# Cosformer attention into a SwiGLU layer on one core: the order of the opening's products, the gates of two load groups, and later loads of q for batch 3

## The chip, the cores and the metric

The kernel runs on one core of a Trainium2 chip. The metric is the device time of one execution in microseconds (us). Before the change it is 332.5 us, the median of 12 runs (331.68 to 333.79).

## What is computed

Attention with linear cost over 8 batches of 8 heads, 576 tokens and 64 features, and then a gated layer on all 4608 tokens:

```python
def phi(x, c, s):
    r = np.maximum(x, 0.0)
    return np.concatenate([r * c, r * s], axis=-1)   # c, s: cosine and sine of the token's place
q_p = phi(q, cos_w, sin_w); k_p = phi(k, cos_w, sin_w)
kv = np.einsum('bhsf,bhsd->bhfd', k_p, v); z = np.sum(k_p, axis=2)
num = np.einsum('bhsf,bhfd->bhsd', q_p, kv)
den = np.einsum('bhsf,bhf->bhs', q_p, z)[..., None] + 1e-06
x = num / den                        # heads side by side: 4608 x 512
xn = x / np.sqrt(np.mean(x * x, -1) + 1e-06) * rms_g
g = xn @ w_gate; val = xn @ w_val    # 512 x 1536
out = (g * sigmoid(g) * val) @ w_out # 1536 x 512
```

## The kernel before, in words

**Stages of a batch.** The 512 first tokens of a batch are handled as four tiles of 128 (the index c or j), the other 64 as a tail (index 4; tails of two batches are joined). `k_phi` and `q_phi` (L219, L231) apply phi on VectorE (V, the cosine half) and ScalarE (A, the sine half). `v_cast` and `v_cast_tail` copy v into bf16, the tail on GpSimd (G). `kvz_pe` (L294) forms kv and z for all heads in the PSUM tile psA, and `kvz_evac` copies them out. phi(q) is transposed, on TensorE with a copy behind it (`q_tr_pe`, `q_tr_evac`, L259, L265) for batches 0 and 1, by a transposing DMA on SyncE's queue for the others (`q_tr_dma`, L254). `nd_pe` (L322) forms numerator and denominator of one tile in psA. `nd_post` (L374) divides them on VectorE. `x_sq` (L389) sums the squares on ScalarE and takes the power -1/2 on GpSimd (rs). `x_norm` (L403) scales on VectorE. x is transposed on TensorE (`x_tr_pe`, `x_tr_evac`, L426, L432) or by DMA (`x_tr_dma`, L423).

**The gated layer.** A block is the 512 first tokens of one batch; a ninth block holds all tails. Block blk has 12 steps n = 0 to 11 (`gval_step`, L715): four products each with w_gate and w_val of 128 output features (`gval_mm`, L440), an activation on ScalarE (`gval_act`), a product on VectorE (`gval_h`, L456). Then come four steps n = 12 to 15 of twelve products with w_out (`out_step`, L724), each copied by ScalarE and stored. psG and psV have two banks each, so TensorE may run one step ahead.

**Order.** Every engine runs its instructions in the order of the program. That order is written out by hand: `at(blk, n, where, f, ...)` (L638) hangs a call into a step, before its products ("pe"), in the middle of them ("mid"), before its activation ("pre") or behind it ("post"). While block b is computed, batch b+1 goes through attention. x of batch 2 is normalised and transposed behind its nd at steps 7, 9, 11 and 12 of block 1 (`nds`, L689). Loads of batch 3 and later are cut in pieces and hung into the steps of the block two earlier (L707 to L713), between the transposing DMAs on SyncE's queue.

**The opening** (L489 to L624). TensorE multiplies a tile of zeros (`filler`, L482) where it has nothing yet. Batch 0 goes through attention tile by tile, and steps 0 to 5 of block 0 are computed in parts of 128 or 256 columns (`open_ffn`, L560, each group of four products accumulating one bank part; `open_h`, L575) as soon as a tile of x is there. Steps 6 to 11 follow (L737). Then the twelve w_out products of all four tiles of block 0 are run together, n by n, with the attention of batch 1 between them (L747 to L779); the product number n needs quarter n // 3 of wo.

**Loads and their gates.** w_gate and w_val are loaded in three slices of columns each by GpSimd's queue (`weight_dmas` 0 to 5, L497 to L506). k, q and v of batch 1 come on SyncE's queue behind weights 4 (L645 to L651). wo comes in four quarters on GpSimd's queue: the first waits for k of batch 1, the second for q of batch 1 (L652 to L657). The q tails of batches 0 and 1 wait for the third quarter, and k, q and v of batch 2 stand behind them on SyncE's queue (L761 to L767).

Of the kernel before, what the change touches and what calls it, by code (L numbers as in the profile page):

```python
# [22 lines left out]
def kernel(  # L23
# [40 lines left out]
    LOW, HIGH = (0, 4), (4, 8)  # L64
# [200 lines left out]
    def q_tr_evac(eng, b, c, bank, heads=(0, 8)):  # L265
        h0, h1 = heads if c < 4 else (0, 4)
        dst = bank.bitcast(BF16).rearrange("p (h s) -> p h s", s=P)
        copy(eng, q_dst(b, c)[:, h0:h1, :], dst[:, h0:h1, :])
# [105 lines left out]
    def nd_post(b, j, pst):  # L374
        o = headview(pst)
        xt = x_tile(b, j)
        rec = four.tile([P, 2, 4], FP32, name="rec", tag="rec")
        nc.vector.tensor_scalar(
            out=rec[:, :, :], in0=o[:, :, :, D], scalar1=1e-6, scalar2=None, op0=ALU.add
        )  # L380
        nc.vector.reciprocal(out=rec[:, :, :], in_=rec[:, :, :])
        nc.vector.tensor_tensor(  # L382
            out=xt[:, 0:DM].rearrange("p (b h d) -> p b h d", b=2, d=D),
            in0=o[:, :, :, 0:D],
            in1=rec[:, :, :].unsqueeze(3).to_broadcast([P, 2, 4, D]),
            op=ALU.mult,
        )

    def x_sq(b, j):  # L389
        xt = x_of[(b, j)]  # L390
        scr = one.tile([P, DM + 1], BF16, name="scr", tag="scr")
        ms = four.tile([P, 1], FP32, name="ms", tag="ms")
        nc.scalar.activation(  # L393
            out=scr[:, :], in_=xt[:, 0 : DM + 1], func=AF.Square,
            scale=1.0 / math.sqrt(DM), accum_out=ms[:, :],
        )
        rs = four.tile([P, 1], FP32, name="rs", tag="rs")
        nc.gpsimd.tensor_tensor(out=rs[:, :], in0=ms[:, :], in1=mhalf[:, :], op=ALU.pow)  # L398
        rs_of[(b, j)] = rs
# [3 lines left out]
    def x_norm(b, j):  # L403
        xn = four.tile([P, DM], BF16, name="xn", tag="xn")
        nc.vector.scalar_tensor_tensor(  # L405
            out=xn[:, :], in0=x_of[(b, j)][:, 0:DM], scalar=rs_of[(b, j)][:, :], in1=gb[:, :],
            op0=ALU.mult, op1=ALU.mult,
        )
        xn_of[(b, j)] = xn
# [16 lines left out]
    def x_tr_pe(b, j, bank):  # L426
        xn = xn_of[(b, j)]
        dst = bank.bitcast(BF16).rearrange("p (t s) -> p t s", s=P)
        for t in range(NDT):
            nc.tensor.transpose(dst[:, t, :], xn[:, t * P : (t + 1) * P], ident[:, :])  # L430

    def x_tr_evac(eng, b, j, bank, part=(0, 4)):  # L432
        dst = bank.bitcast(BF16).rearrange("p (t s) -> p t s", s=P)
        copy(eng, x_dst(b, j)[:, part[0] : part[1], :], dst[:, part[0] : part[1], :])
# [47 lines left out]
    def filler(n, bank):  # L482
        for _ in range(n):
            nc.tensor.matmul(bank, lhsT=warm[:, 0:P], rhs=warm[:, :], start=True, stop=True)  # L484
# [75 lines left out]
    def open_ffn(pair, steps, c0, c1, base=0, parts=(0, 1)):  # L560

        x = xnT[0]
        for i, n in enumerate(steps):
            for a in parts:
                w = (wg, wv)[a]
                bank = pairs[pair][a]
                lo = base + 256 * i + c0 % 256
                for t in range(NDT):
                    nc.tensor.matmul(  # L569
                        bank[:, lo : lo + c1 - c0],  # L570
                        lhsT=w[:, t, n * P : (n + 1) * P], rhs=x[:, t, c0:c1],
                        start=(t == 0), stop=(t == NDT - 1),
                    )
# [17 lines left out]
    x_norm(0, 1)  # L591
    open_ffn(0, (0, 1), 0, 128)
    x_tr_pe(0, 1, psV[1][:, :])
    x_tr_evac(A, 0, 1, psV[1][:, :])
    q_tr_evac(V, 0, 3, psO[1][:, :])
    nd_pe(0, 2, psA)
    nd_post(0, 2, psA)
    x_sq(0, 2)
    filler(2, psG[1][:, :])
    open_ffn(0, (0, 1), 128, 256)  # L600
    open_ffn(1, (2, 3), 0, 256, parts=(0,))
    nd_pe(0, 3, psA)
    nd_post(0, 3, psA)
    x_norm(0, 2)
    open_ffn(2, (4, 5), 0, 256, parts=(0,))
    open_h(0, 0, 0)
    x_sq(0, 3)
    x_tr_pe(0, 2, psA[:, 0, :])
    x_tr_evac(A, 0, 2, psA[:, 0, :])
    open_ffn(1, (2, 3), 0, 256, parts=(1,))  # L610
    x_norm(0, 3)
    open_h(1, 2, 0)
    open_ffn(2, (4, 5), 0, 256, parts=(1,))
    open_ffn(0, (0, 1), 256, 384)
    x_tr_pe(0, 3, psA[:, 1, :])
    x_tr_evac(A, 0, 3, psA[:, 1, :])
    open_h(2, 4, 0)
    filler(1, psA[:, 0, :])
    open_ffn(0, (0, 1), 384, 512)
    open_h(0, 0, 1)  # L620
    open_ffn(1, (2, 3), 256, 512)
# [28 lines left out]
    load_main("v", v, 1, HIGH)  # L650
    load_tail("v", v, 1)  # L651
    w = wo_load(0)  # L652
    tc.add_manual_dep(w.ins, d.ins.name, SYNC_DEP, reason="after k of batch 1")
    w = wo_load(1)
    tc.add_manual_dep(w.ins, gate_q.ins.name, SYNC_DEP, reason="after q of batch 1")
    wo_load(2)
# [1 line left out]


    for c in range(5):  # L660
        at(0, 8 + c // 3, "post", k_phi, V, 1, c, 0)
        at(0, 8 + c // 3, "post", k_phi, A, 1, c, 1)
    for c in range(3):
        at(0, 10 + c // 2, "post", q_phi, V, 1, c, 0)
        at(0, 10 + c // 2, "post", q_phi, A, 1, c, 1)
    at(0, 11, "post", v_cast_tail, G, 1)


    for nb in range(2, B):
        b = nb - 1  # L670
        late = nb == 2
        vb, vn = (b, 3) if late else (b - 1, 14)
        if late:
            at(vb, vn, "post", v_cast, V, nb, LOW)
        for c in range(5):
            kb, kn = (b, (1, 1, 1, 1, 2)[c]) if late else (b - 1, 12 + (c * 3) // 5)
            if not late or c > 1:
                at(kb, kn, "post", k_phi, V, nb, c, 0)
            if not late or c > 0:
                at(kb, kn, "post", k_phi, A, nb, c, 1)  # L680
            qn = (2, 3, 5, 5, 6)[c] if late else c
            at(b, qn, "post", q_phi, V, nb, c, 0)
            at(b, qn, "post", q_phi, A, nb, c, 1)
            at(b, qn, "post", q_tr_dma, nb, c)
        if not late:
            at(vb, vn, "post", v_cast, V, nb, LOW)
        at(vb, vn + 1, "post", v_cast, V, nb, HIGH)
        at(vb, vn, "post", v_cast_tail, G, nb)
        kz, nds = (6, (7, 9, 11, 12)) if late else (4, (5, 7, 9, 11))  # L689
        at(b, kz, "pe", kvz_pe, nb, psA)  # L690
        at(b, kz, "pre", kvz_evac, A, nb, psA, 0)
        at(b, kz, "pre", kvz_evac, A, nb, psA, 1)
        for j in range(4):
            n = nds[j]
            at(b, n, "mid" if n == NNT else "pe", nd_pe, nb, j, psA)
            at(b, n, "pre", nd_post, nb, j, psA)
            at(b, n, "post", x_sq, nb, j)
            where = "pre" if n + 1 >= NNT else "post"
            at(b, n + 1, where, x_norm, nb, j)
            at(b, n + 1, where, x_tr_dma, nb, j)  # L700
        if nb % 2 == 1:
            at(b, 13, "pe", nd_pe, nb, 4, psA)
            at(b, 13, "pre", nd_post, nb, 4, psA)
            at(b, 13, "post", x_sq, nb, 4)
            at(b, 14, "post", x_norm, nb, 4)
            at(b, 14, "post", x_tr_dma, nb, 4)
    for nb in range(3, B):  # L707

        b = nb - 2
        for i, which in enumerate(("k", "v", "q")):  # L710
            for p in range(5):
                n = (0, 6, 10)[i] + p if b == 1 else 5 * i + p
                at(b, n, "post", load_piece, which, nb, p)  # L713

    def gval_step(blk, n, bank=None):  # L715
        bank = n % 2 if bank is None else bank
# [25 lines left out]
        x_tr_pe(1, j, bank)  # L742
        x_tr_evac(A, 1, j, bank)

    qbank = [psA[:, 0, :], psV[0][:, :], psV[1][:, :], psA[:, 0, :]]
    nd_at = {4: 0, 6: 1, 8: 2, 9: 3}
    for n in range(NNT - 2):  # L747
        for c in ((0, 1), (2,), (3,))[n] if n < 3 else ():
            q_tr_pe(1, c, qbank[c])
            q_tr_evac(V if c % 2 else A, 1, c, qbank[c])  # L750
        if n == 0:
            q_phi(V, 1, 3, 0)
            q_phi(A, 1, 3, 1)
        if n == 1:
            v_cast(A, 1, LOW)
            v_cast(V, 1, HIGH)
        if n == 3:
            kvz_pe(1, psA)
            kvz_evac(A, 1, psA, 0)
            kvz_evac(V, 1, psA, 1)  # L760
            for bb in (0, 1):  # L761
                d = load_tail("q", q, bb)
                if bb == 0:
                    tc.add_manual_dep(d.ins, wo_dmas[2].ins.name, SYNC_DEP, reason="after wo")
            load("k", 2)
            load("q", 2)
            load("v", 2)  # L767
        if n == 7:
            x_norm(1, 0)
        if n == 9:  # L770
            x_norm(1, 1)
            tr1(0, psV[0][:, :])
        if n in nd_at:
            j = nd_at[n]
            nd_pe(1, j, psA)
            nd_post(1, j, psA)
            x_sq(1, j)
        for j in range(4):
            out_mm(0, j, n, banks0[j])  # L779
# [89 lines left out]
```

## Time and profile before

| | us |
|---|---|
| median of 12 runs | 332.5 |
| the profiled execution | 332.48 |
| its span in the trace | 330.3 |
| TensorE busy in the span | 320.7 |
| VectorE, ScalarE, GpSimd busy | 181.6, 168.5, 37.7 |
| first step of block 0 with 512 columns (n = 6) starts | 34.13 |
| first w_out product of block 0 | 45.39 |
| block 1 starts, with half of the columns | 60.07 |
| block 2 starts | 96.29 |

The trace gives the start and length of every instruction in us from the start of the span, and, in brackets, how long the engine stood idle before it and what ended that. A row "x8" is eight instructions in a chain; their ends overlap, so the price of one is read from the start of the next row: four products of 512 columns take 0.86, four of 256 columns 0.44, four of 128 columns 0.22, the eight of an nd 0.26, one filler 0.22. L74 and L85 are lines of load helpers, L255 and L424 the transposing DMAs of phi(q) and of x, L272 and L274 copies on ScalarE and on VectorE or GpSimd, L474 the store of an output tile.

### The profile page before, as it was taken

The page shows a single profiled execution, that of the slowest core. Times are in us where ns is not written, and L with a number is a line of the kernel's source. Part 1 is how long each engine was busy: PE and PEld are TensorE (multiplying, and loading weights), DVE is VectorE, ACT ScalarE, POOL GpSimd, SP SyncE. Part 2 cuts the span into 40 slices and gives each one's busy share as a digit, 9 for nine tenths or more (in the row PEclk, how much of TensorE's full clock was granted, in tenths as well). Part 3 has the DMA queues.
Part 4 walks back from the last instruction along what each step waited for, and adds up shares of the span by engine and source line. Part 5 has one row for each costly group of instructions (what it writes and reads, how often), then busy time and mean ns, then how long its engine had stood idle before and what let it go on. Part 6 is the DMA issues. An engine that isn't in the chain of part 4 may idle for free.

```text
span 330.3 us, 5951 instructions
## 1 busy us (share of the span) xinstructions
PE 320.7 (97%) x2191; PEld 163.7 (50%) x2191; DVE 181.6 (55%) x376; ACT 168.5 (51%) x326; POOL 37.7 (11%) x83
## 2 busy tenths in 40 slices
PE   8988999999989999999999999999999999999995
PEld 3567555654435444544454445444544444444443
DVE  3775576877755774577257755674567234204410
ACT  4554593785556556645564466536654233223321
POOL 3520311101200111012001110120001000000000
PEclk9999999999999999999999999999999999999999
DMA  7999997999699966876678777967631310020013
GB/s 209 282 192 254 307 198 223 321 198 222 155 268 206 193 167 191 209 173 194 203 165 202 180 216 186 197 154 238 134 67 32 116 45 0 2 110 17 0 34 96
DMA packets 95117, 54.14 MB, mean 164 GB/s; under 512 B 60016, under 2 KB 90480, under 8 KB 95088
## 3 DMA queue, kind: packets, MB, share of 16 engines
q1 hardware_dynamic: 89072, 48.65, 58.1%
q0 software_dynamic: 4768, 4.72, 8.7%
q10 hardware_dynamic: 1248, 0.39, 0.6%
q8 instruction: 17, 0.28, 0.3%
q14 instruction: 12, 0.10, 0.1%
HBM read 38.01 MB, written 9.44 MB: 144 GB/s over the span
## 4 chain that ended last, share of the span: by engine, by line
PE 86%; DVE 5%; DMA 4%; issue 2%; ACT 2%; POOL 0%; SPq 0%; ACTq 0%; DVEq 0%
PE psG L444 25%; PE psV L444 25%; PE psC L464 23%; PE psA L300 3%; DMA rq<-in_q_dram 2%; PE psA L328 2%; PE psG L464 1%; DVE xt L382 1%; DMA xnT<-xn 1%; PE psG L569 1%; DVE xn L405 1%; PE psV L569 1%; PE psO L569 1%; PE psG L484 1%; ACT scr L393 1%
## 5 line engine op out<-in xcount | busy, mean ns | idle before, releaser
L459 DVE TENSOR_TENSOR hT<-psV,sg 128x512 bf16<-128x512 f32 x102 | 70.3, 690 | 98.6 <-PE psV L444 87.3
L453 ACT ACTIVATE sg<-psG 128x512 f32<-128x512 f32 x102 | 60.6, 594 | 67.0 <-PE psG L444 66.8
L444 PE MATMUL psG<-xnT,wg 128*128 128x512 bf16 (+1 forms) x368 | 92.7, 375 | 1.5 <-DMA xnT<-xn 1.4
L444 PE MATMUL psV<-xnT,wv 128*128 128x512 bf16 (+1 forms) x368 | 92.7, 375 | 0.0
L464 PE MATMUL psC<-wo,hT 128*128 128x512 bf16 x396 | 89.4, 380 | 0.0
L444 PEld LDWEIGHTS <-wv 128*128 128x128 bf16 x416 | 40.6, 98 | 47.4
L464 PEld LDWEIGHTS <-hT 128*128 128x128 bf16 x420 | 40.2, 98 | 46.4
L444 PEld LDWEIGHTS <-wg 128*128 128x128 bf16 x416 | 38.5, 98 | 42.4 <-issue 1.9
L398 POOL TENSOR_TENSOR rs<-ms,mhalf 128x1 f32<-128x1 f32 x36 | 19.8, 549 | 191.0 <-ACT scr L393 191.0
L272 ACT COPY osb<-psC 128x512 f32<-128x512 f32 (+1 forms) x33 | 19.1, 578 | 43.5 <-PE psC L464 42.8
L393 ACT ACTIVATE scr<-xt 128x513 bf16<-128x513 f32 x36 | 22.8, 635 | 26.3 <-DVE xt L382 25.7
L405 DVE SCALAR_TENSOR_TENSOR xn<-xt,rs,gb 128x512 bf16<-128x512 f32 x36 | 27.3, 757 | 15.0 <-POOL rs L398 14.9
L382 DVE TENSOR_TENSOR xt<-psA,rec 128x512 f32<-128x512 f32 x35 | 24.2, 691 | 1.2
L213 ACT ACTIVATE qp<-rq,tab 128x512 bf16<-128x512 f32 x32 | 22.6, 714 | 1.3 <-DMA rq<-in_q_dram 1.2
L213 ACT ACTIVATE kpm<-rk,tab 128x512 bf16<-128x512 f32 (+1 forms) x34 | 21.2, 676 | 0.5 <-DMA rk<-in_k_dram 0.4
L215 DVE TENSOR_SCALAR kpm<-rk,tab 128x512 bf16<-128x512 f32 (+1 forms) x38 | 15.5, 460 | 4.3 <-ACT tab L168 3.3
L215 DVE TENSOR_SCALAR qp<-rq,tab 128x512 bf16<-128x512 f32 x32 | 15.1, 478 | 0.9 <-DMA rq<-in_q_dram 0.9
L484 PE MATMUL psG<-warm 128*128 128x512 bf16 x50 | 14.4, 434 | 1.2 <-DVE fidx L150 1.2
L328 PEld LDWEIGHTS <-qpT 128*128 128x128 bf16 x248 | 11.9, 98 | 6.9 <-issue 0.6
L328 PE MATMUL psA<-kvzs,qpT 128*128 128x65 bf16 x248 | 12.9, 194 | 0.2
L444 PE MATMUL psG<-xnt_tail,wg 128*128 128x512 bf16 x48 | 12.3, 380 | 0.0
L444 PE MATMUL psV<-xnt_tail,wv 128*128 128x512 bf16 x48 | 12.3, 379 | 0.0
(98 smaller groups left out, 194.1 us busy)
## 6 DMA issues: line engine op xcount, KB each, us to landing
out_dram<-osb SPq DMA_DIRECT2D x32, 256.0 KB, 2.5
rk<-in_k_dram SPq DMA_DIRECT2D x20, 256.0 KB, 3.3
rv<-in_v_dram SPq DMA_DIRECT2D x20, 256.0 KB, 3.1
rq<-in_q_dram SPq DMA_DIRECT2D x20, 256.0 KB, 3.2
rk<-in_k_dram SPq DMA_DIRECT2D x2, 1024.0 KB, 7.1
rq<-in_q_dram SPq DMA_DIRECT2D x2, 1024.0 KB, 9.5
rv<-in_v_dram SPq DMA_DIRECT2D x3, 512.0 KB, 9.9
wo<-in_moe_w_out_dram POOLq DMA_DIRECT2D x4, 384.0 KB, 8.6
```

The costliest lines, as they stand in the source:

```text
L213: nc.scalar.activation(out=out_ap, in_=in_ap, func=AF.Relu, scale=scale)
L215: eng.tensor_scalar(out=out_ap, in0=in_ap, scalar1=scale, scalar2=0.0, op0=ALU.mult, op1=ALU.max)
L272: nc.scalar.copy(out=o, in_=i)
L328: nc.tensor.matmul(o[:, g, i, :], lhsT=qpT[(b, 0)][:, h, j * P : (j + 1) * P], rhs=kvzs[(b, g)][:, i * E : (i + 1) * E], start=True, stop= ...
L382: nc.vector.tensor_tensor(out=xt[:, 0:DM].rearrange("p (b h d) -> p b h d", b=2, d=D), in0=o[:, :, :, 0:D], in1=rec[:, :, :].unsqueeze(3). ...
L393: nc.scalar.activation(out=scr[:, :], in_=xt[:, 0 : DM + 1], func=AF.Square, scale=1.0 / math.sqrt(DM), accum_out=ms[:, :],)
L398: nc.gpsimd.tensor_tensor(out=rs[:, :], in0=ms[:, :], in1=mhalf[:, :], op=ALU.pow)
L405: nc.vector.scalar_tensor_tensor(out=xn[:, :], in0=x_of[(b, j)][:, 0:DM], scalar=rs_of[(b, j)][:, :], in1=gb[:, :], op0=ALU.mult, op1=ALU. ...
L444: nc.tensor.matmul(pst[bank][:, cols[0] : cols[1]], lhsT=w[:, t, n * P : (n + 1) * P], rhs=x[:, t, cols[0] : cols[1]], start=(t == 0), sto ...
L453: nc.scalar.activation(out=sg[:, :], in_=psG[bank][:, :], func=AF.Silu)
L459: nc.vector.tensor_tensor(out=hTs[blk][:, n, :], in0=psV[bank][:, :], in1=sg[:, :], op=ALU.mult)
L464: nc.tensor.matmul(bank, lhsT=hTs[blk][:, n, j * P : (j + 1) * P], rhs=wo[:, n, :], start=(n == 0), stop=(n == NNT - 1),)
```

## The change

Five things, all in the order of work.

In the opening, the emptying of the transposes of q tile 3 and x tile 1 swap engines, one filler of two goes, nd of tile 3 moves ahead of the first products of steps 2 and 3, the second half of those products moves ahead of the transposes of x tile 2, the products of columns 256 to 384 move behind the transposes of x tile 3, and the filler there goes.

The first quarter of wo waits for the last weights instead of k of batch 1. The q tails, with batch 2's loads behind them, wait for the second quarter of wo instead of the third.

In batch 1, phi of k and q moves back by up to one step of block 0, and the transposes of q move from ahead of the w_out products n = 0, 1, 2 to ahead of n = 1 to 4.

In batch 3, the five pieces of q are loaded from step 13 of block 1 to step 1 of block 2 instead of steps 10 to 14 of block 1. Its q_phi and transposes come two steps later, and its nd one step later.

```diff
     x_tr_pe(0, 1, psV[1][:, :])
-    x_tr_evac(A, 0, 1, psV[1][:, :])
-    q_tr_evac(V, 0, 3, psO[1][:, :])
+    q_tr_evac(A, 0, 3, psO[1][:, :])
+    x_tr_evac(V, 0, 1, psV[1][:, :])
     nd_pe(0, 2, psA)
     nd_post(0, 2, psA)
     x_sq(0, 2)
-    filler(2, psG[1][:, :])
+    filler(1, psG[1][:, :])
     open_ffn(0, (0, 1), 128, 256)
-    open_ffn(1, (2, 3), 0, 256, parts=(0,))
     nd_pe(0, 3, psA)
     nd_post(0, 3, psA)
+    open_ffn(1, (2, 3), 0, 256, parts=(0,))
     x_norm(0, 2)
     open_ffn(2, (4, 5), 0, 256, parts=(0,))
     open_h(0, 0, 0)
     x_sq(0, 3)
+    open_ffn(1, (2, 3), 0, 256, parts=(1,))
     x_tr_pe(0, 2, psA[:, 0, :])
     x_tr_evac(A, 0, 2, psA[:, 0, :])
-    open_ffn(1, (2, 3), 0, 256, parts=(1,))
     x_norm(0, 3)
     open_h(1, 2, 0)
     open_ffn(2, (4, 5), 0, 256, parts=(1,))
-    open_ffn(0, (0, 1), 256, 384)
     x_tr_pe(0, 3, psA[:, 1, :])
     x_tr_evac(A, 0, 3, psA[:, 1, :])
     open_h(2, 4, 0)
-    filler(1, psA[:, 0, :])
+    open_ffn(0, (0, 1), 256, 384)
     open_ffn(0, (0, 1), 384, 512)
...
     w = wo_load(0)
-    tc.add_manual_dep(w.ins, d.ins.name, SYNC_DEP, reason="after k of batch 1")
+    tc.add_manual_dep(w.ins, weight_dmas[5].ins.name, SYNC_DEP, reason="after the weights")
...
     for c in range(5):
-        at(0, 8 + c // 3, "post", k_phi, V, 1, c, 0)
-        at(0, 8 + c // 3, "post", k_phi, A, 1, c, 1)
-    for c in range(3):
-        at(0, 10 + c // 2, "post", q_phi, V, 1, c, 0)
-        at(0, 10 + c // 2, "post", q_phi, A, 1, c, 1)
+        at(0, 8 + (c + 1) // 3, "post", k_phi, V, 1, c, 0)
+        at(0, 8 + (c + 1) // 3, "post", k_phi, A, 1, c, 1)
+    for c in range(2):
+        at(0, 11, "post", q_phi, V, 1, c, 0)
+        at(0, 11, "post", q_phi, A, 1, c, 1)
...
-            qn = (2, 3, 5, 5, 6)[c] if late else c
+            qn = (2, 3, 5, 5, 6)[c] if late else c + 2 * (nb == 3)
...
-        kz, nds = (6, (7, 9, 11, 12)) if late else (4, (5, 7, 9, 11))
+        kz, nds = (6, (7, 9, 11, 12)) if late else (4, (6, 8, 10, 12) if nb == 3 else (5, 7, 9, 11))
...
-                n = (0, 6, 10)[i] + p if b == 1 else 5 * i + p
-                at(b, n, "post", load_piece, which, nb, p)
+                n = (0, 6, 13)[i] + p if b == 1 else 5 * i + p
+                at(b + n // 16, n % 16, "post", load_piece, which, nb, p)
...
-    qbank = [psA[:, 0, :], psV[0][:, :], psV[1][:, :], psA[:, 0, :]]
+    qbank = [psV[0][:, :], psV[1][:, :], psV[0][:, :], psV[1][:, :]]
     nd_at = {4: 0, 6: 1, 8: 2, 9: 3}
     for n in range(NNT - 2):
-        for c in ((0, 1), (2,), (3,))[n] if n < 3 else ():
-            q_tr_pe(1, c, qbank[c])
-            q_tr_evac(V if c % 2 else A, 1, c, qbank[c])
         if n == 0:
-            q_phi(V, 1, 3, 0)
-            q_phi(A, 1, 3, 1)
-        if n == 1:
-            v_cast(A, 1, LOW)
-            v_cast(V, 1, HIGH)
+            for c in (2, 3):
+                q_phi(V, 1, c, 0)
+                q_phi(A, 1, c, 1)
         if n == 3:
             kvz_pe(1, psA)
             kvz_evac(A, 1, psA, 0)
             kvz_evac(V, 1, psA, 1)
+        if 1 <= n <= 4:
+            c = n - 1
+            q_tr_pe(1, c, qbank[c])
+            q_tr_evac(V if c < 2 else A, 1, c, qbank[c])
+        if n == 2:
+            v_cast(A, 1, LOW)
+            v_cast(V, 1, HIGH)
+        if n == 3:
             for bb in (0, 1):
                 d = load_tail("q", q, bb)
                 if bb == 0:
-                    tc.add_manual_dep(d.ins, wo_dmas[2].ins.name, SYNC_DEP, reason="after wo")
+                    tc.add_manual_dep(d.ins, wo_dmas[1].ins.name, SYNC_DEP, reason="after wo")
```

## The prediction

> **What bounds the kernel now.** I read the page's busy rows first, then TensorE's waits, then those waits in the timelines of TensorE, SyncE and VectorE, and last the transfers of the opening.
>
> ```profile
> PE 320.7 (97%) x2191; PEld 163.7 (50%) x2191; DVE 181.6 (55%) x376; ACT 168.5 (51%) x326; POOL 37.7 (11%) x83
> ...
> PEclk9999999999999999999999999999999999999999
> ```
>
> TensorE is busy for 320.7 of 330.3 us at the full granted clock. So only work taken off TensorE, or one of its waits, can be gained. These are all its waits:
>
> ```profile
> PE psG L444 <- DMA xnT<-xn: 1.4, 1, 1.4
> PE psG L484 <- DVE fidx L150: 1.2, 1, 1.2
> PE psA L430 <- DVE xn L405: 1.0, 1, 1.0
> PE psA L484 <- ACT xnT L272: 0.7, 1, 0.7
> PE psO L263 <- DVE qp L215: 0.6, 1, 0.6
> PE psV L263 <- ACT qp L213: 0.4, 1, 0.4
> ```
>
> The change can reach three: 1.0 and 0.7 in the opening, 1.4 at the start of block 2. In TensorE's timeline (start, us, then the wait in brackets):
>
> ```profile
> 25.60 0.40 PE L430 MATMUL psA<-ident,xn 128*128 128x128 bf16 x4 [1.01 <-DVE xn L405]
> ...
> 29.53 0.38 PE L484 MATMUL psA<-warm 128*128 128x512 bf16 x1 [0.67 <-ACT xnT L272]
> 29.75 0.39 PE L569 MATMUL psG<-xnT,wg 128*128 128x128 bf16 x4
> ```
>
> SyncE's queue ahead of the 1.4 us (the transposes L424 at 89.72 and 92.18 are those of tiles 2 and 3 of batch 2; loads of q for batch 3 stand before each), and VectorE's normalised tile 3, done at 90.11:
>
> ```profile
> 87.29 2.33 SPq L74 DMA_DIRECT2D rq<-in_q_dram  x2
> 89.72 1.23 SPq L424 DMA_TRANSPOSE xnT<-xn  x1
> 91.06 0.55 SPq L474 DMA_DIRECT2D out_dram<-osb  x1
> 91.66 0.42 SPq L74 DMA_DIRECT2D rq<-in_q_dram  x1
> 92.18 1.29 SPq L424 DMA_TRANSPOSE xnT<-xn  x1
> ```
> ```profile
> 89.36 0.75 DVE L405 SCALAR_TENSOR_TENSOR xn<-xt,rs,gb 128x512 bf16<-128x512 f32 x1 [0.71 <-POOL rs L398]
> ```
>
> **The opening, by steps** (times in the clock of the run before). The second filler at 21.17 goes (0.22). The transpose of tile 1 is now emptied by VectorE (its row for the same copy of tile 0: 0.42) instead of ScalarE (0.58 from 20.90); it can start at 20.9, so the next products start at 21.37, not 21.54. They take 0.88. nd of tile 3 then wants psA at 22.25, but nd_post of tile 2 now begins after that copy: 21.28 plus its 1.12 (21.16 to 22.28 before), so 22.42: a new wait of about 0.15. After it: nd 0.26 to 22.68; three groups of eight products, 0.87 each, to 25.29. x of tile 2 is normalised by then: nd_post 22.8 to 23.9, x_norm 0.74 to 24.65. So the 1.01 us stall is covered by the group of wv products that now stands ahead of it. Transposes 0.22, eight products 0.88, transposes of tile 3 0.22 (its x, behind rs at 25.4, is ready at 26.2, needed at 26.39) to 26.61. Eight products on columns 256 to 384, which need tile 2 alone, take 0.88 to 27.49 and cover ScalarE's copy of tile 3 (after an activation, done at 27.45). They stand where the wait of 0.67 and a filler of 0.22 stood. The products of columns 384 to 512 start at about 27.5 instead of 29.75: **-2.2 us**. The last weights, landed at 31.6 (issue 16.0 plus 15.6), are needed at 32.8, no wait.
>
> **Block 0 and batch 1, where the opening's gain must survive.** Steps 6 to 11 end at 42.3 instead of 44.49. What was there in time by a small margin:
>
> - wo's first quarter was issued at 35.72 and landed 8.5 later, 44.2; its first product began at 45.39. Now the product comes at 42.3, since the transposes of q moved behind it. At the old gate that would be a wait of 1.9. The new gate opens at 31.6. GpSimd has nothing else queued there until the v tails (44.4), so the earlier wait holds up nobody.
>
> How soon it lands is the disputed cost. The windows (last column GB/s):
>
> ```profile
> 22.00:26.00 4.00, 2.99 (x41) 2.54 (x39) 2.46 (x6) 1.93 (x5) 0.75 (x2) 1.00 1.18 209
> 28.00:31.00 3.00, 2.33 (x37) 2.06 (x35) 0.69 (x1) 1.47 (x3) 0.00 (x0) 1.00 1.14 226
> ...
> 38.00:41.00 3.00, 3.00 (x15) 1.37 (x14) 1.97 (x4) 2.35 (x5) 1.73 (x3) 1.00 1.13 317
> 42.00:44.00 2.00, 2.00 (x11) 0.88 (x10) 1.86 (x5) 2.00 (x5) 0.00 (x0) 1.00 1.24 219
> ```
>
> Weights move at about 209. k of batch 1 is issued at 27.56, yet the rate stays near the weights' (226) until they are in; wo is issued at 35.72, yet 38 to 41 runs at 317, the rate of q, k and v loads, and only then falls to 219. So older transfers go first. The Trainium skill (DMA: Bandwidth & Descriptors, Queues, rings and completion order) says that each engine takes turns between its queues. By that rule wo would take its share from k at once: land near 36, push q from 39.0 to about 40.9, and with q the gate of the second quarter (lands 48.1, needed 47.9). By the rows it comes behind the first half of v (issued 30.6, landed 40.5): 384 KB at 209 GB/s are 1.9 us, so 42.4 alone, 43.2 if it shares as before (2.7 us). I take the rows: 42.8, a wait of 0.5. Bounds: 0 (8.5 us after its issue, 40.2) to 0.9.
>
> - q_phi moves from step 10 to 11, and four stand before the first copies. VectorE ends h of step 11 at 43.1 and q_phi of c=0 at 43.65 (rows 0.69, 0.48, overlapping 0.1); TensorE wants it after four products (0.86), 43.2: 0.4 alone, but inside the wait of 0.5 if that occurs. Under the turn-taking rule this 0.4 and 0.2 for the second quarter replace the 0.5: the sum hardly moves.
> - kvz at 46.3: the second v tail is cast at 46.5, its first use is half way in, 47.0. All transfers ahead of that tail are the same bytes, so I take 0; up to 1.4 if wo's 1.9 us push it to 48.4.
> - k_phi is at most one step later; k landed at 35.5 and ScalarE asks at 37. Nothing.
> - Batch 2's gate: SyncE waits for the second quarter (39.27 + 7.2 = 46.5), not the third (48.7). TensorE is 1.7 us ahead, so margins stay (k of batch 2: landed 57.0, used 62.4). Nothing either way.
>
> Stage: **+0.5**.
>
> **Block 1's end.** Three loads of q (2.33 and 0.42 of SyncE) leave the places before the transposes. Tile 2's then goes at about 87.3, and tile 3's when VectorE is done, 90.15. Transposes around landed in 3.5, 4.0, once 4.9: 93.7 to 95.05. TensorE needs it at 94.85. **-1.4** (bounds -1.44, -1.2).
>
> **Batch 3, which pays for it.** Its q now comes behind outputs and the tail's transpose: the last piece issues near 97.9 and lands 3.3 to 4.0 later, 101.2 to 101.9. q_phi of c=0, at step 2, would start at 101.4, its transpose goes at 102 and lands 3.3 later, 105.3; nd of tile 0, moved to step 6, needs it at 106.4. Margin 1.1; at 5.2 us, the longest qp transpose near there, 0.8 would be lost. I take **+0.2**. The last x of batch 3 is one step later: nd at the middle of step 12, its transpose landing about 8.1 after that, needed 9.7 after: no loss.
>
> **Sum.** -2.2 + 0.5 - 1.4 + 0.2 = -2.9. The profiled execution took 332.48 (span 330.3, 2.2 outside it), the median of the twelve runs is 332.5, so the sum holds for both: **329.6 us**. About 0.2% (0.7 us) is what such measurements can tell from no change.
>
> **Rivals.**
>
> 1. A wait takes the place of the one removed, at kvz: the v tail comes behind wo. For it: wo jumps ahead of v's second half. Against: the same bytes in total. 1.4 more: 331.0. Chance 0.14.
> 2. SyncE wasn't what held tile 3's transpose, or it lands as late for traffic. For: one took 4.9. Against: 2 us between x_norm's end and its issue. The 1.4 is not gained: 331.0. Chance 0.12.
> 3. Slower: ScalarE and VectorE stand at step 2 of block 2 for batch 3's last q piece, with the activation of step 3 queued behind. TensorE has two banks, so it is held once the piece lands after 103.4 (activation of q 0.71 and of step 3 0.60, step 5 due at 104.7); each us later is a us. At the 9.9 us that loads took behind a backlog, it lands at 107.8, 4.4 late: 332.5 - 2.9 + 4.4 = 334.0. It outweighs the gains by 0.7 from a landing at 107.0 (9.1 after issue). For: it is last in a full queue. Against: loads there landed in 3.6 to 4.0. Chance 0.09.
> 4. The change doesn't do what it says: psA is freed so late that nd of tile 3, and all behind it, gains nothing, and wo's wait eats the rest; only part of the 1.4 stays: 332.2. Chance 0.07.
>
> The forecast has 0.58. Faster by over 0.2% (below 331.8): 0.58 + 0.14 + 0.12 = 0.84; within: 0.07; slower: 0.09. **Range:** the forecast's own bounds give 328.8 (332.5 - 2.2 - 1.44, with no wait for wo and none in batch 3) to 330.6; with rivals 1 and 2 up to 331.7. That leaves about 0.16 out.
>
> **What would show it.** TensorE's waits without the 1.0 and 0.7; the first block-0 step of 512 columns at 31.9 instead of 34.13; a wait up to 0.9 on wo or q_phi near 42.5; block 2 starting about 3 us earlier without the DMA wait; no wait at nd in block 2. Wrong if TensorE waits over 1 us near 46 (kvz), at block 2's step 5 or 6, or if the 1.4 stays.

## The result, and the profile after

The changed kernel takes 329.15 us, the median of 8 runs (328.93 to 329.76), against 332.42 us in 32 runs of the kernel before: a ratio of 0.9904, 95% interval 0.9893 to 0.9915, so 2.8 to 3.6 us less. The forecast was 329.6.

The profiled execution took 329.79 us, with a span of 327.6; the eight others took 328.93 to 329.76. Where each stage starts, from TensorE's timelines:

| start, us | before | after | difference |
|---|---|---|---|
| first step of 512 columns in block 0 | 34.13 | 32.06 | -2.07 |
| block 1 | 60.07 | 58.34 | -1.73 |
| block 2 | 96.29 | 92.96 | -3.33 |
| block 3 | 130.08 | 127.32 | -2.76 |
| ninth block (tails) | 295.35 | 292.59 | -2.76 |
| end of the span | 330.3 | 327.6 | -2.7 |

So the opening gives 2.07, batch 1 takes back 0.34, the end of block 1 gives 1.60, block 2 takes back 0.57, and from block 3 on nothing differs. TensorE's waits in the changed kernel (us in total, times, longest):

```profile
PE psG L484 <- DVE fidx L150: 1.2, 1, 1.2
PE psO L263 <- DVE qp L215: 0.6, 1, 0.6
PE psV L263 <- DVE qp L215: 0.6, 1, 0.6
PE psV L263 <- ACT qp L213: 0.4, 1, 0.4
PE psA L328 <- DMA qpT<-qp: 0.3, 1, 0.3
```

The three waits that the change could reach (1.0, 0.7, 1.4) are gone. Two are new: 0.6 on VectorE's phi of q (psV, L263) and 0.3 at nd on a transpose of phi of q (psA, L328). TensorE's timeline (start, us, engine, line, operation, and the wait in brackets) shows where:

```profile
25.46 0.39 PE L430 MATMUL psA<-ident,xn 128*128 128x128 bf16 x4
...
26.56 0.39 PE L430 MATMUL psA<-ident,xn 128*128 128x128 bf16 x4
26.78 0.39 PE L569 MATMUL psG<-xnT,wg 128*128 128x128 bf16 x4
...
32.06 1.03 PE L444 MATMUL psG<-xnT,wg 128*128 128x512 bf16 x4
...
44.02 0.61 PE L263 MATMUL psV<-ident,qp 128*128 128x128 bf16 x8 [0.57 <-DVE qp L215]
...
92.96 1.03 PE L444 MATMUL psG<-xnT,wg 128*128 128x512 bf16 x4
...
108.80 0.43 PE L328 MATMUL psA<-kvzs,qpT 128*128 128x65 bf16 x8 [0.33 <-DMA qpT<-qp]
```

The transposes of x tiles 2 and 3 (25.46, 26.56) have no bracket any more, nor has the start of block 2 (92.96). SyncE's queue ahead of block 2:

```profile
86.25 1.35 SPq L424 DMA_TRANSPOSE xnT<-xn  x1
87.71 1.53 SPq L474 DMA_DIRECT2D out_dram<-osb  x1
89.35 1.23 SPq L424 DMA_TRANSPOSE xnT<-xn  x1
```

No load of q stands there. The transpose of tile 3 goes at 89.35 and lands 3.5 later, at 92.85, just before TensorE wants it.

### The profile page after: what moved, and what is told of

It is laid out like the page before. It is cut to its first block, busy times and chain, and to the rows that moved or that the text cites. A ratio compares the mean times of both kernels' runs of the same rounds, so it can differ in the third digit from the quotient of the medians.

```text
span 327.6 us, 5943 instructions
## 1 busy us (share of the span) xinstructions
PE 320.2 (98%) x2189; PEld 163.4 (50%) x2189; DVE 181.6 (55%) x376; ACT 168.7 (51%) x326; POOL 37.5 (11%) x83
## 4 chain that ended last, share of the span: by engine, by line
PE 89%; DMA 5%; DVE 2%; ACT 1%; issue 1%; SPq 0%; DVEq 0%; ACTq 0%
PE psC L464 26%; PE psG L444 25%; PE psV L444 25%; DMA rq<-in_q_dram 4%; PE psA L328 2%; PE psA L300 2%; DMA qpT<-qp 2%; PE psG L464 1%; PE psG L569 1%; PE psV L569 1%; PE psO L569 1%; PE psV L263 1%; PE psG L484 1%; PE psO L263 1%; PE psA L335 0%
## 5 line engine op out<-in xcount | busy, mean ns | idle before, releaser
L328 PEld LDWEIGHTS <-qpT 128*128 128x128 bf16 x248 | 11.7, 98 | 7.2 <-DMA qpT<-qp 1.2
L328 PE MATMUL psA<-kvzs,qpT 128*128 128x65 bf16 x248 | 13.0, 194 | 0.5 <-DMA qpT<-qp 0.3
```

The lines of the kernel that those rows point to most:

```text
L328: nc.tensor.matmul(o[:, g, i, :], lhsT=qpT[(b, 0)][:, h, j * P : (j + 1) * P], rhs=kvzs[(b, g)][:, i * E : (i + 1) * E], start=True, stop= ...
```

## The experiments

Theory: each gain is one wait of TensorE at its own place, and the gains add up. Rivals: the earlier gate of wo carries the first gain; and at block 2 the bytes of the q loads, not their places in SyncE's queue, held the transposes. Differences in time below are between ratios to the kernel before, measured beside each kernel on the same chip, times 332.4. Rows are those of one profiled execution of each kernel.

**The opening undone.** The block of the opening is that of before, the rest as changed:

```diff
...
     open_ffn(0, (0, 1), 128, 256)
+    open_ffn(1, (2, 3), 0, 256, parts=(0,))
     nd_pe(0, 3, psA)
     nd_post(0, 3, psA)
-    open_ffn(1, (2, 3), 0, 256, parts=(0,))
...
```

> The changed kernel with the opening of the kernel before (order of products, both fillers); the gates and batch 3 stay as changed. Theory A, the gains are single waits of TensorE and add up: the first step of 512 columns is back near 34.1 instead of 32.06, the wait of 0.57 on phi of q near 43 is kept or shrinks (q is in at 41.3, steps are 2 us later), block 2 starts 2.0 later, in all +1.9 us over the changed kernel, near 331.0. Theory B, the earlier gate of wo carries the first gain, so the order alone is worth little: less than +0.7, below 329.9.

Measured: 331.76 us, ratio 0.9976 (0.9966 to 0.9985), 2.4 more than the changed kernel. Block 2 starts at 94.93, 1.97 later, as theory A had it. In the profiled execution (332.60 us, above the median) the rest is a longer wait in block 2, at nd of batch 3:

```profile
106.98 0.43 PE L328 MATMUL psA<-kvzs,qpT 128*128 128x65 bf16 x8 [0.32 <-DMA qpT<-qp]
...
111.52 0.43 PE L328 MATMUL psA<-kvzs,qpT 128*128 128x65 bf16 x8 [0.66 <-DMA qpT<-qp]
```

Two waits here, 0.33 in the changed kernel, and no bracket in the six other profiles with this order of batch 3. But a gap can be too small for a bracket, so the length of block 2 is the better measure. Of the eight profiles, four have 33.8, as before; the others have 0.2, 0.6 (the changed kernel), 0.8 and 1.3 (this one) more. It is a thin margin that comes and goes, not a fixed price.

**The opening alone**, in the kernel before:

> The kernel before with the opening's new order of products alone; gates, batch 1 and batch 3 as before. Theory A: the first step of 512 columns starts 2.0 earlier; wo's first quarter still lands near 44.2, and its first product, two transposes of q later than in the changed kernel, is asked for near 43.3, so 0.9 to 1.3 is given back in a new wait on wo; the 1.4 at block 2 stays: -0.9 to -1.2 against before, near 331.4. Theory B (worth nothing without the gate): 332.4.

Measured: 330.83 us, ratio 0.9957 (0.9944 to 0.9970), 1.4 less than before. The profiled execution is the fastest of its five (330.04, so 2.4 less than the one before). TensorE's timeline:

```profile
31.96 1.03 PE L444 MATMUL psG<-xnT,wg 128*128 128x512 bf16 x4
...
43.97 0.60 PE L464 MATMUL psC<-wo,hT 128*128 128x512 bf16 x2 [0.60 <-DMA wo<-in_moe_w_out_dram]
...
94.15 1.02 PE L444 MATMUL psG<-xnT,wg 128*128 128x512 bf16 x4 [0.70 <-DMA xnT<-xn]
```

By these rows the opening is worth 2.17 us by itself (31.96 instead of 34.13). With the old gate 0.6 is given back on wo (0.9 to 1.3 expected). The wait at block 2 is 0.7 here instead of 1.4, in a kernel that was not meant to touch it: the transpose of tile 3 goes 1.1 after its x is ready instead of 2.1. Why is not settled. SyncE issued the two q pieces ahead of it in 1.43 instead of 2.33 us, but so it did where batch 3 was undone (1.44), with a wait of 1.39. The median gained 1 us less than this execution; which of the two waits is longer in the others is not known.

**The first gate undone:**

```diff
-    tc.add_manual_dep(w.ins, weight_dmas[5].ins.name, SYNC_DEP, reason="after the weights")
+    tc.add_manual_dep(w.ins, d.ins.name, SYNC_DEP, reason="after k of batch 1")
```

> The changed kernel with the first quarter of wo again behind k of batch 1. Theory A: wo lands near 44 and TensorE, which asks at 42.4, waits 1.5 there; phi of q is then no longer late, so 0.7 of it is cancelled: +0.8, near 330.0. By the order-of-issue reading of the prediction q of batch 1 would land as in the changed kernel (41.3); if the two queues take turns, q lands near 39.3, about 2 us sooner than in the changed kernel. Theory B (the gate carries the first gain): +2, near 331.2.

Measured: 330.64 us, ratio 0.9957 (0.9944 to 0.9969), 1.8 more. In this profile TensorE waits for wo:

```profile
32.42 1.03 PE L444 MATMUL psG<-xnT,wg 128*128 128x512 bf16 x4
...
44.72 0.61 PE L464 MATMUL psC<-wo,hT 128*128 128x512 bf16 x2 [1.77 <-DMA wo<-in_moe_w_out_dram]
```

From row to row the wait is 1.94 (44.72 less 42.78, where the products of step 11 end), and the 0.74 on phi of q is gone, so the gate is worth 1.2 in these rows (0.8 expected). Another 0.36 came earlier (32.42 against 32.06), most of it a wait of 0.31 for w_val, at 20.05, which is none of the gate's. The run also answers the disputed cost. On GpSimd's queue the last three quarters of wo start when q has landed, in the changed kernel:

```profile
32.30 0.78 POOL L511 DMA_DIRECT2D wo<-in_moe_w_out_dram  x1 [6.88 <-DMA wv<-in_moe_w_val_dram]
41.33 2.31 POOL L511 DMA_DIRECT2D wo<-in_moe_w_out_dram  x3 [8.24 <-DMA rq<-in_q_dram]
```

and with the old gate:

```profile
36.23 0.78 POOL L511 DMA_DIRECT2D wo<-in_moe_w_out_dram  x1 [10.45 <-DMA rk<-in_k_dram]
39.78 2.40 POOL L511 DMA_DIRECT2D wo<-in_moe_w_out_dram  x3 [2.77 <-DMA rq<-in_q_dram]
```

q was issued at 30.49 and 30.83. Counted to these rows, it lands 10.8 us after its issue when wo comes early and 9.0 when wo comes late. The other profiles agree: by the trace's own landing times, 9.8 to 11.6 in the ten with the new gate, 8.7 to 9.4 in the four with the old one. So wo, issued 1.8 us behind q, cost it 1.9 us: they shared the DMA engines, and the order of issue did not decide. The rate in the changed kernel (last column, GB/s) shows when:

```profile
35.00:37.00 2.00, 2.00 (x11) 0.88 (x9) 0.69 (x1) 0.87 (x2) 0.00 (x0) 1.00 1.11 302
37.00:39.00 2.00, 2.00 (x11) 0.91 (x10) 1.48 (x3) 2.00 (x5) 0.00 (x0) 1.00 1.18 260
39.00:41.00 2.00, 2.00 (x11) 0.94 (x10) 1.74 (x4) 2.00 (x4) 0.00 (x0) 1.00 1.13 291
```

With the old gate (wo issued at 36.23), the rate from 37 to 39 is still that of the other loads. In the kernel before it stays there until 40 and then falls:

```profile
37.00:39.00 2.00, 2.00 (x11) 0.94 (x10) 1.13 (x3) 2.00 (x4) 0.01 (x1) 1.00 1.10 349
```
```profile
36.00:40.00 4.00, 4.00 (x21) 1.80 (x19) 1.80 (x3) 1.95 (x4) 1.23 (x2) 1.00 1.10 348
40.50:42.00 1.50, 1.50 (x9) 0.68 (x7) 1.44 (x4) 1.50 (x3) 1.27 (x2) 1.00 1.21 215
```

By half microseconds the fall begins 4 to 5 us after wo is issued, in all fourteen profiles: near 37 with the new gate (issued at 32.30), near 40 with the old one (35.72 before). wo lands 8.3 to 9.1 after its issue with either gate.

**The second gate undone** (the q tails wait for the third quarter of wo again):

```diff
-                    tc.add_manual_dep(d.ins, wo_dmas[1].ins.name, SYNC_DEP, reason="after wo")
+                    tc.add_manual_dep(d.ins, wo_dmas[2].ins.name, SYNC_DEP, reason="after wo")
```

> The changed kernel with the q tails, and so batch 2's loads, again behind the third quarter of wo. Theory A: margins of batch 2 are several us, so nothing changes in TensorE's waits, 329.0 to 329.4. Rival: the gate gives a part of the gain; without it a wait on batch 2's phi or kvz shows in block 1, +0.5 or more.

Measured: 329.75 us, ratio 0.9912 (0.9889 to 0.9935), not to be told from the changed kernel. No wait of TensorE came with it. The gate moves batch 2's loads by 1.5 us: k of batch 2 is issued at 51.40 here and at 49.90 in the changed kernel. Against the kernel before (50.68) only 0.8 is left, because q, and behind it the second quarter of wo, land later.

**The fillers back:**

```diff
-    filler(1, psG[1][:, :])
+    filler(2, psG[1][:, :])
...
     open_ffn(0, (0, 1), 256, 384)
+    filler(1, psA[:, 0, :])
     open_ffn(0, (0, 1), 384, 512)
```

> The changed kernel with both fillers back, the second one between the products of columns 256 to 384 and 384 to 512. The fillers compute nothing that is used. By the prediction's sum they cost 0.43. By the row of the changed kernel the first lies in a wait of 0.27 on the copy of x tile 1 and costs nothing, so the first step of 512 columns is 0.2 later and the time 329.2 to 329.4.

Measured: 329.45 us, ratio 0.9907 (0.9884 to 0.9930), no difference that the times can tell. The rows tell: with both fillers the next products start at 21.50,

```profile
21.01 0.59 PE L484 MATMUL psG<-warm 128*128 128x512 bf16 x2
21.50 0.38 PE L569 MATMUL psG<-xnT,wg 128*128 128x128 bf16 x4
```

and with one filler (in the run below with nd of batch 3 later, which has the changed opening and whose rows start at the same time) also at 21.50:

```profile
21.01 0.38 PE L484 MATMUL psG<-warm 128*128 128x512 bf16 x1
21.50 0.38 PE L569 MATMUL psG<-xnT,wg 128*128 128x128 bf16 x4
```

The first filler lies in the wait for the copy of x tile 1 and costs nothing. Only the second (0.22) does: the first step of 512 columns is at 32.23 instead of 32.00.

**Batch 3's later q undone**, and **alone** in the kernel before. The same lines, each way:

```diff
-            qn = (2, 3, 5, 5, 6)[c] if late else c + 2 * (nb == 3)
+            qn = (2, 3, 5, 5, 6)[c] if late else c
...
-        kz, nds = (6, (7, 9, 11, 12)) if late else (4, (6, 8, 10, 12) if nb == 3 else (5, 7, 9, 11))
+        kz, nds = (6, (7, 9, 11, 12)) if late else (4, (5, 7, 9, 11))
...
-                n = (0, 6, 13)[i] + p if b == 1 else 5 * i + p
+                n = (0, 6, 10)[i] + p if b == 1 else 5 * i + p
```

> The changed kernel with the loads, phi, transposes and nd of batch 3 at the steps of before. Theory A: the wait at the start of block 2 comes back (1.44 in brackets, 1.6 from row to row) and the wait of 0.33 at nd in block 2 goes: +1.1 to +1.3, near 330.4. Rival, the wait at block 2 went because TensorE and the batch 2 loads moved, not because of the q loads: no change, 329.2.

> The kernel before with batch 3's later q alone (loads, phi, transposes, nd). Theory A: the wait of 1.4 at block 2 goes (1.6 from row to row), 0 to 0.8 comes back at nd in block 2: -0.8 to -1.6, near 331.2. Rival (it needs the opening or the gate too): 332.4.

Measured: undone 330.74 us, ratio 0.9951 (0.9938 to 0.9964), 1.6 more than the changed kernel; the wait at block 2 is back:

```profile
94.34 1.02 PE L444 MATMUL psG<-xnT,wg 128*128 128x512 bf16 x4 [1.39 <-DMA xnT<-xn]
```

Alone 330.92 us, ratio 0.9960 (0.9948 to 0.9972), 1.3 less than before; the wait is gone and none comes in block 2:

```profile
94.63 1.03 PE L444 MATMUL psG<-xnT,wg 128*128 128x512 bf16 x4
```

So it needs neither opening nor gate. The opening alone and this alone add up to -2.8; with the gates it is -3.2, the same within the intervals.

**The q loads of batch 3 on ScalarE's queue**, at the steps of before: SyncE's queue is free of the four main pieces, the bytes are the same.

```diff
             load_main(
-                which, src_of[which], b, (2 * p, 2 * p + 2), two if which == "k" else one
+                which, src_of[which], b, (2 * p, 2 * p + 2), two if which == "k" else one,
+                nc.scalar if which == "q" and b == 3 else nc.sync,
             )
```

> The changed kernel with batch 3 at the steps of before, but its four main q pieces issued on ScalarE's queue, so that SyncE's queue is free of them while the same bytes move at the same time. Theory A (SyncE's order holds the transposes): no wait at the start of block 2, no wait in block 2 either, 328.7 to 329.2. Rival (traffic holds them): the wait of about 1.4 stays, near 330.4. If issuing costs ScalarE more than its idle time, activations come late and a new wait of TensorE shows.

Measured: 330.93 us, ratio 0.9958 (0.9946 to 0.9971), 1.8 more than the changed kernel. SyncE and TensorE:

```profile
88.11 1.97 SPq L425 DMA_TRANSPOSE xnT<-xn  x1
```
```profile
94.08 1.02 PE L445 MATMUL psG<-xnT,wg 128*128 128x512 bf16 x4 [1.26 <-DMA xnT<-xn]
```

Tile 3 was normalised at 88.08 and its transpose issued at 88.11, without any delay, and yet it landed 5.8 us later, where the changed kernel's took 3.5. The transpose of tile 2 took 6.1 against 4.1. Theory A fell here: with the bytes of q in flight beside them, the transposes are late however early SyncE issues them. The windows show the load (the column before the last is the busy share of the DMA engines). In this kernel:

```profile
86.00:88.00 2.00, 2.00 (x25) 0.94 (x24) 1.29 (x3) 2.00 (x5) 0.55 (x1) 1.00 1.36 244
88.00:90.00 2.00, 2.00 (x11) 0.88 (x10) 1.93 (x7) 1.60 (x3) 0.07 (x1) 1.00 1.17 66
```

In the changed kernel:

```profile
86.00:88.00 2.00, 2.00 (x25) 0.94 (x24) 1.29 (x4) 1.75 (x4) 0.90 (x2) 1.00 0.56 120
88.00:90.00 2.00, 2.00 (x11) 0.94 (x10) 1.93 (x6) 1.91 (x4) 0.75 (x1) 1.00 0.66 47
```

**Small loads in the places of the q pieces**: SyncE's queue is occupied, few bytes move.

```diff
+    spare = one.tile([P, 4, D], FP32, name="spare")
+    def load_spare(i):
+        nc.sync.dma_start(
+            out=spare[:, i, :], in_=q[3, 0, 0:512, :].rearrange("(p j) d -> p j d", j=4)[:, i, :]
+        )
...
+    for i in range(3):
+        at(1, 10 + i, "post", load_spare, i)
```

> The changed kernel with three small loads (32 KB each, of data nobody reads) on SyncE's queue at steps 10, 11 and 12 of block 1, where the q pieces of batch 3 stood before (256 KB each). It adds work that the reference does not need. Theory S, SyncE's issue order held the transposes: the transposes of tiles 2 and 3 are issued about as late as before and a wait of 0.7 to 1.4 is back at block 2, near 330.2. Theory T, the bytes ahead of them on the DMA engines held them (as in the run with q on ScalarE's queue, where issue was on time and landing took 5.8): no wait or under 0.3, 329.2 to 329.5.

Measured: 330.11 us, ratio 0.9941 (0.9923 to 0.9959), 1.2 more than the changed kernel. Of this the rows at block 2 explain 0.5, and 0.2 came earlier (first step of 512 columns at 32.25 instead of 32.06, behind a first wait on q of 1.5 instead of 0.4); the rest is not explained. SyncE and TensorE:

```profile
86.85 0.35 SPq L95 DMA_DIRECT2D spare<-in_q_dram  x1
87.31 1.85 SPq L430 DMA_TRANSPOSE xnT<-xn  x1
...
90.36 1.19 SPq L430 DMA_TRANSPOSE xnT<-xn  x1
```
```profile
93.82 1.02 PE L450 MATMUL psG<-xnT,wg 128*128 128x512 bf16 x4 [0.35 <-DMA xnT<-xn]
```

The result lies between the two theories. Tile 3's transpose goes 1.5 after its x is ready (88.85), but lands in 3.3. So for that transpose:

| | x ready | issued after | landed after issue | wait of TensorE |
|---|---|---|---|---|
| before | 90.11 | 2.07 | 4.0 | 1.44 |
| q pieces on ScalarE's queue | 88.08 | 0.03 | 5.8 | 1.26 |
| small loads on SyncE | 88.85 | 1.5 | 3.3 | 0.35 |
| changed | 88.50 | 0.85 | 3.5 | none |

Each row is one profile. Moving the loads was right for two reasons at once. In the kernel before, their places in the queue cost about 1.2 (2.07 less 0.85) and the landing 0.5 (4.0 less 3.5). Freeing the places alone takes only 0.18 off the wait: the transposes go sooner, but beside the bytes of q, and land 2.3 later (5.8 less 3.5). Taking most of the bytes away and keeping the places takes 1.09 off it, in part because SyncE is also done with small loads sooner (1.5 instead of 2.07). Only moving both leaves no wait.

**Two attempts at the new waits.** Phi of q tile 0 one step earlier:

```diff
-        at(0, 11, "post", q_phi, V, 1, c, 0)
-        at(0, 11, "post", q_phi, A, 1, c, 1)
+        at(0, 10 + c, "post", q_phi, V, 1, c, 0)
+        at(0, 10 + c, "post", q_phi, A, 1, c, 1)
```

> The changed kernel with phi of q tile 0 of batch 1 at step 10 instead of 11. Theory A, the wait of 0.57 on phi of q (0.74 from row to row) is VectorE's order alone: it goes, kvz does not wait: -0.6, near 328.6. Rival, q itself lands too late (41.3) and phi at step 10 holds the activation of step 11, or kvz waits for the v tail instead: 0 to -0.2.

Measured: 328.93 us, ratio 0.9896 (0.9883 to 0.9909). The intervals of this and of the changed kernel overlap, but the wait is gone from TensorE's list, and block 2 starts at 92.43 instead of 92.96:

```profile
PE psG L484 <- DVE fidx L150: 1.2, 1, 1.2
PE psV L263 <- ACT qp L213: 0.6, 1, 0.6
PE psO L263 <- DVE qp L215: 0.6, 1, 0.6
```

And nd of batch 3 at steps 7, 9, 10, 12 instead of 6, 8, 10, 12, alone and with the former:

> The changed kernel with nd of batch 3 at steps 7, 9, 10, 12 instead of 6, 8, 10, 12. Theory A, the waits at nd in block 2 (0.33 in the changed kernel's profile, 1.0 in the run with the old opening, none in some others) are transposes of phi of q that land too late: they go, 0 to -0.5, 328.7 to 329.2. Rival, the later x of batch 3 makes block 3 wait instead: +0.3 or more.

> The changed kernel with phi of q tile 0 of batch 1 at step 10 and nd of batch 3 at steps 7, 9, 10, 12. Theory A: both waits gone and additive, -0.6 to -1.0 against the changed kernel, 328.2 to 328.6. Rival: only the first counts, 328.9.

Measured: 329.90 us, ratio 0.9917 (0.9893 to 0.9941), and with both 329.13 us, ratio 0.9904 (0.9878 to 0.9929). No gain; the wait changed its place, in both:

```profile
112.67 0.41 PE L328 MATMUL psA<-kvzs,qpT 128*128 128x65 bf16 x8 [0.57 <-DVE xt L382]
```

Tile 2's nd now comes one step after tile 1's and waits for VectorE to read psA, which none of the two expectations had.

## Why the prediction was right, point by point

- **Opening, -2.2.** Measured -2.07, of which 0.10 is an earlier start (the first transposes behind the fillers at 17.77 instead of 17.87). The cover worked as written, and the foreseen wait of 0.15 on psA is there (nd of tile 3 at 22.38, the products before it done at 22.23). Another 0.21 ahead of the wv products at 24.58 was not foreseen: the weight load of that row waited for w_val. Of the ten other profiles with this opening only one has it (that with the first gate undone). The opening alone, without it and with the start of before, gave -2.17.
- **Batch 1, +0.5.** Measured +0.34, but the step on wo failed. wo was not waited for: issued at 32.30, it landed 9.1 later, at 41.4, a microsecond ahead of its use. That is neither the 42.8 taken from the rows nor the 36 that the prediction drew from the rule of turns; only the lower bound, counted as 8.5 us from the issue, had the form that the profiles show (8.3 to 9.1). The reading that older transfers go first came from two rows that do not need it. The 317 of 38 to 41 is the mean over the fall from 348 to 215, which came when wo's bytes did, 4.5 us after its issue. k, issued at 27.56, shows from 30.5 on (272), 1.1 us before the last weights had landed. Once wo's bytes moved, its queue and that of q shared the engines, as the Trainium skill (DMA: Bandwidth & Descriptors, Queues, rings and completion order) says: the rate fell to 260 and q landed at 41.3 instead of the 39.0 of the step. This cost TensorE nothing here. It waited for phi of q, 0.57 in brackets and 0.74 from row to row, but VectorE reached it only at 43.30, behind the product of step 11, two microseconds after q was in:

```profile
43.30 1.75 DVE L215 TENSOR_SCALAR qp<-rq,tab 128x512 bf16<-128x512 f32 x4
```

  With phi one step earlier this wait is gone, though q lands as late (41.2). The prediction had it as 0.4 "alone". So the sum survived because both readings gave nearly the same, as the prediction said, and by luck: two gaps of the kernel before (0.24 ahead of kvz at 49.11, 0.23 ahead of nd at 51.41, too small for brackets) closed unforeseen. With 0.08 more inside kvz, 0.74 + 0.08 - 0.47 = 0.35, the measured 0.34 within rounding.
- **kvz, 0.** Right: the v tails were cast at 45.9, kvz started at 46.64, without a wait. Only its second half was 0.08 late; VectorE's copy of v ended just before it (47.27). The first rival (331.0) fell.
- **Batch 2's gate, nothing.** Right in effect (the run with it undone shows no wait), wrong in size: batch 2's loads came 0.8 sooner than before, not 2.2.
- **Block 1's end, -1.4.** Measured -1.60. The size was right, the reason half: the sum let SyncE's order alone hold the transpose, and the run on ScalarE's queue shows that with the places free the bytes still hold it. The second rival named traffic; it was wrong only because the change moved the bytes as well.
- **Batch 3, +0.2.** Measured +0.57 in this profile, at tile 1, which the sum did not follow, and not at tile 0. Over the eight profiles with this order block 2 lost 0 to 1.3, 0.36 in the mean. The transpose took 5.3 us, about the 5.2 that set the bound. The chain of waits shows the whole path, load, phi, and the transpose:

```profile
95.99 4.57 DMA rq<-in_q_dram
...
103.47 5.29 DMA qpT<-qp
```

  ScalarE stood 2.64 us for that load, at the place of the third rival. It landed at 100.56; the limit of 103.4, in the prediction's clock with block 2 at 94.85, is 101.5 here. So the slower case was 0.9 us away, not impossible.
- **Sum.** -2.9 foreseen. The profiled execution gives -2.7, the medians -3.2; the profiled execution was slower than the other eight, and it has the wait in block 2 that half of the profiles with this order lack.

## What to carry to other kernels

A wait's bracket is not its whole price: take the start of the next row less the time at which it would have followed, and look for gaps too small for a bracket. When a load stands ahead of a transfer that matters, it delays it by its place in the issuing queue and by its bytes on the DMA engines; moving it to another queue removes only the first. Opening a gate earlier is paid by the transfers in flight at that moment, so cost their consumers as well as the one that was waiting.

## What was not expected of the hardware

The bracket of a wait is short by about 0.17 us: at the start of block 2 before, the last product's row ends at 94.84 (89.49 plus 5.35), while 24 products at 0.216 end their turn at 94.67, 1.62 before the next row; the bracket says 1.44, and the stage got 1.60 shorter.

The DMA transposes of x tiles 2 and 3 of batch 2, one size and one place, took from 2.5 to 6.1 us to land in these kernels. For tile 3 it was 2.5 to 3.6 where no q piece stood ahead, 3.7 to 4.0 behind q pieces in the same queue, and 5.8 beside q pieces on the other queue.

A load's bytes do not show in the rate as soon as it is issued. For k of batch 1 it took 2 to 3 us, for wo 4 to 5, in every profile, so that a queue can look held back by older transfers without being so. Where the first gate was undone, the rate even fell to 127 GB/s from 30.0 to 30.5, with k issued at 28.63. Here this delay is enough to account for the rows from which the prediction read that older transfers go first. Why it is longer for wo was not settled; no run issued wo with the DMA engines empty.
